# A conformer block on one core: another hand-fixed order for the first nine tenths of its instruction blocks, and the XN and AN clearings issued by VectorE

## The chip, the core and the metric

The kernel runs on one core of one Trainium2 chip. The time is that of one launch on the device, in microseconds (us). Before the change three runs gave 881.92, 882.08 and 883.56 us, median 882.08 us. The profile is that of one further execution of the same program.

In the text PE is TensorE (PEld its weight loads, which overlap its matmuls), ACT is ScalarE, DVE is VectorE, POOL is GpSimd and SP is SyncE, which here only issues DMAs.

## The reference, cut to what matters

Two sequences of 4000 tokens with 144 features go through one conformer block. All inputs are bf16.

```python
def reference(x, w_ff1a, w_ff1b, w_qkv, w_o, w_pw1, dw, w_pw2, w_ff2a, w_ff2b):
    B, T, D = x.shape                       # 2, 4000, 144; 4 heads of 36
    x = x + 0.5 * (_silu(_layernorm(x) @ w_ff1a) @ w_ff1b)
    qkv = _layernorm(x) @ w_qkv
    ...
    p = _softmax(jnp.einsum('bhqd,bhkd->bhqk', q, k) * scale, axis=-1)
    att = jnp.einsum('bhqk,bhkd->bhqd', p, v)
    ...
    x = x + att @ w_o
    h = _layernorm(x) @ w_pw1
    h = h[..., :D] * _sigmoid(h[..., D:])
    ...                                     # c: depthwise convolution over 5 tokens
    x = x + _silu(c) @ w_pw2
    x = x + 0.5 * (_silu(_layernorm(x) @ w_ff2a) @ w_ff2b)
    return _layernorm(x)
```

The softmax over 4000 keys for 4 heads and 8000 tokens is most of the work: 128 million exponentials.

## The kernel before

The 8000 tokens are cut into 16 chunks of 500, each of 4 blocks of 125 rows; 8 chunks make a sequence. Keys are cut into tiles of 64 rows, 62 full ones and one of 32 for a sequence. For a chunk of queries and a tile of keys, four matmuls on quarters of the PE array (64 rows by 64 columns; lines `PS<-QT,KT`) make scores for 4 heads in a pair of PSUM banks. ACT turns the pair into exponentials with one instruction (`PT<-PS 128x1000`). For every fifth tile or so DVE does it instead, with five instructions (two `PT<-PS 128x500`, two `PT<-PT` as integers, one product). Then four more quarter matmuls (`PS<-PT,VA`) multiply by the values and add up in two further banks. Six banks are left for scores and for all else.

Around this run, chunk by chunk: the first feed-forward layer, and the keys, values and queries, for the first sequence before and during its attention (the "front", the first 88 us or so); the rest for the second sequence beside the attention of the first; behind each chunk's attention the output projection, the gated convolution and the second feed-forward layer; at the end (the "tail", from some 836 us) what is left of the last chunks. A layer norm takes its statistics on DVE (`ST<-X`), the power -1/2 and, for most chunks, the normalisation itself on POOL (`RS`, `XN<-X,RS`). Its result XN is transposed on DVE in squares, written by SP's DMA queue to a scratch tensor `rows` and read back as XT or XTQ. XN and AN (the normalised and the attention rows, 5 and 4 buffers of 640 columns) have columns beyond the 576 that are ever written, and the transposes read them, so each buffer is cleared before its first use; so is the lower part of XT (5 buffers), 80 rows of which 16 come by DMA.

The order of all this is not left to a scheduler on the chip. The kernel's Python first emits operations greedily with a table of estimated costs; each decision of that loop is a step, and the operations of one engine in one step are a block. `Rec.reorder` (line 279) then moves the blocks of each engine: `ORDER` (line 38) is a string for each engine, in which a character says by how many places a block moves from its emitted place. `PLACES` (line 111) says, tile by tile, which of the six banks a PSUM tile takes; there are 1724 tiles. After that the semaphore waits are derived from the data dependencies in the final order (`Rec.finish`, line 344). So the four compute engines run four fixed lists, in order, that wait for each other by semaphores only: an instruction that waits holds up everything behind it on its engine.

The lines of the trace are nearly all those of `Rec.replay` (398), which issues every operation; groups are told apart by their tiles.

The clearings before: `ln` (line 1068) clears the 64 columns that matter on POOL at the first use of an XN buffer by halves of a chunk, and the whole buffer at its first use by a whole chunk; `setup_dw` (line 930) clears all AN at once on POOL when the front ends; `transp` (line 1038) clears XT's lower part on POOL at its first use by DMA. An emitted clearing also moves the greedy loop's clock on by its estimated cost, so that leaving it out would change what is emitted after it.

Of the kernel before, what the change touches and what calls it, by code (L numbers as in the profile page):

```python
# [39 lines left out]
        "PPPPPPQOQOPPPPPRPNPPQQQQLPPQORPNPRPTMORNNVO~OLNOMrMMNPMMNNNOMNNNOPLMQMMMNNPMMNSMNLMMOOPNSOMQMSPNOPU["  # L40
        "OMNRMOPPQIRMSNPNePNOOOcNNNNNNNNNOOLbNLOOQNSH]MMOLOMPMMOOOVPNOOOOPPPTOOOTPMUQMSLNNQQNQOQQNPPPPPTPPROK"
        "PPPPPPPPPPPP`PPPQKVPPKPPMPPRPUPPPROQQQRZOQQQRRKQRRSJPRRRRRRRWSZRNYUR~NHQ@R[KEGOOOPPPPKQOPPSPPSLPQMTP"
        "PPLQQQMPPPQVPPQOX_PTOPPCRTQQRGSQIQQSQRNV8OOQNNVSNOOLOPUUNN_MMWLNNRMMMMOOOPPPPPPQQNPPRSNRSSSORRVTR[OR"
        "AKQ@PPLOOQQNPPPPPUOOOOOPQOPPPPPUOOOOQRPLU`NNNXMMPNLQMNLZRNL`MN_YLLMK`KMNLILNQJMOOOPNYOPNOOOQNNZ^NNNN"
        "OOPNQNQOYP]CNNNNOMPMSO[NKOOQNVMPMMN`NbYMMMMNOMNIcLLNL[MMMNNQNRMJQLLROQSPLRNOQOPUQOMPQMPPRPVPLQOMQNPQ"
        "QQQSKPQSQKQQQQJPPPPPWQQSPKKQQUPPPSWPQRPQAVPPPQCVPQRPWHSYPHSOPQYPQEPQCPRZUPPSOOHDPR^OKOOOOPNOOOO^NOQN"
        "NOOOSNNNNS[NNNdRMNRKYNJWJNNNNNNGOOPP^YNNNNOMNNNNRNNPPPVROOLOOPPRZNNOOOOOPNOSOPNRPSMOOPQOQWNRPRLLNSZP"
        "NPQOIOQOTPPPRPQ]P^USPMMQIQKQQ8QTQQGMRRTQQKRRRRGLRSOMRPQQQJQQRPVP[OOOQEROO^IOQLNOOPPTTOMNQ[FOQNPPSPPM"
        "HPQOQQUPLOPNVPNOOSQNLUOOPNOXPPPLTQNLMPPPQOPPTOOPTPLOOQRNOPPPQOVPNOOOORZOP[PPMOOFRZOL[ROQKQTUBOKNFPPP"
        "_OOOOOOPNOOOOWNNVNNXMNTKMNOMZQOSLNOMSPSLLTPMOOUOPNOOTQOMOPPPQOPPPQOPPPTTQOSQSSSSNEEPQOPTPTMOMORSNNOP"  # L50
        "ROYPQOPQ^NPNPQOPAOOOOOSOOOPPPQQNPPPPPPXOOOOOOOaNPPPLOOOPUMOOOO[IOOPSOOQNPHPSWOOPPPPQGPPPPQQQMPPQQNPQ"
        "O_OOOPZOOOPI_NNNNZOPEOQWP^HKPHSJOLNOO`VPMRJOM^J`MPNKUNLUGNLJQNRIOPPRXOMOOOOPXMOPPMOOOPWOOPPPTKNOOPPP"
        "PPPPPPPQRPSYSQNQYZPRRRADIOXQGVOPJOORPIPPRRSSMR]MHOOQQQVRKNHPLPPPPPPPPPPRZQSQRRbHSGNQGPPQRRGLPQKQQQQJ"
        "QOQRPMQOPPQOSQNRMTROTNPXQQQEPJOQNPRPN_OPPPLRSOPLPPPGPPPSeOMPPQRJZPKLNNNN`NOKOVJNNNNcM`LMMMNNN]MNL]LL"
        "LLLLTWLXKMMVNQ_LMOPPQQ>MOOOTOMRbMMOOOOOTOOOQZIOPJMOOcOMPPT[PRORPEVHOPYCJQOQQGMOQQNQWNQNPPLSP_OaOOOPN"
        "PDPPPLOHPPQLPPPPQOTPNWNPPPWJNPPP`OIOPPPPPPPUQOELRP^TTQOZUPPCGOPQDJPPPPPPRPQWPRURPMFQQ_RPXDPQJLPNOJPN"
        "PPPPPSPPQ`PPTQQRERPQIQTNDPTPPJOPQQNPPUOPPSLPMPPRPQQRPJP[RNQQLaRJQSS[IQMGQQRPCZJPQOPQTPP@RPIPPPPQQQSS"
        "VXUQGNTQSSETDS`OQSCJQQdLOINQMRLLZMNSMMMMZLWPK]JMNLMTLNNNNVN`NNNNNROOPPJQOPLRPRMOQQRPLPXQQQRPTUQHFPQJ"
        "PPPPPPSPROUSPPTLPUOCOPNQOPROTWPRWRPVRZOY^YEOOPPMQ:;QDQQQQQQQQQEQQQMQOROVSMOTTQLVHROTRGNTVPHRPTRaJSQE"
        "QRSKNRNOQOPWQO=OOPNYOOOQNNOO]QOL_PNRO^NOUIPNK_MMW>MMMZMMMM]MMQLMMSNNOMOPPSOVNNPNXNPQOKQOQLQQQQUPPPHO"  # L60
        "QORPQMQOPQQSQOUVWNWMNOKOAOQOPPPPZWNNNOOLNNR^MNVNOMNNNNPSMN]NTNNNNNaNNNOQLN[RNOMRNHMSOSNPQGPQOPRXRPQW"
        "KOHOPPQYPPZPQRCO[I^NORFNNIZMMMNOWLNNNQMNRORRO_KPNOOOYNNNNNNOU^NSUHNKOJNOSOOQRJUPROTYMHNNURNNTMIPNQOU"
        "OOV[MNLNNNPYTNeJLNORNNGOO[]NNNNIQLMRLNRWOPUOO]OM`QO;LSOLO]JOJPRLLMRUNZMOVR[NPDOT^OOOFOSTOMNOSbPQLPRS"
        "_MORR_NPP^OHCNNNOZOWL~NHLMMNNNSOOXNOQQNSSOIVKPNPN]NOOOOOPPVOOOITNPPLPPQOWPPMRPNTKOOTNOPUMOOOQN`OOOPN"
        "OOPPPLOZOQQMPIQO^YROQQRLENO_PNPPPTQNNOROOSVO]QMNRNOPWTNOMNSOPQXbOOOQ[NO~NCdIMMMMMMMfbKMMMQMMJLMPLMUM"
        "MMNL^TR^JSLJQJUKPNLHQMPP`UNNNNOMOOOOPNOOPPPPQQNPQQQMUQQMSOPTQOPTPQUNQSPSQ<TRSSVEQQQHQQFPPPPPQSPMYTOL"
        "NNTMNNNP^[NOMNNQMMOLNN]PNOOR[OPKQN_ZLNESMOOKHOM[NPPLPNOOPPMQSTMNPQQQQRSQRRTCQVNGRNOMTTTMMNUPPQHNQSPM"
        "YVTQKLLSSOIJPSSPTMKORNOQOPPPPPPSORNSMRNRRRNQQRPFRPQQQQQQRPFQO"
    ),
    "act": (  # L70
        "PPPPPPPPPPPPPRSNNOSOOOPPPPPPPUPNOXNNOOOOOQNPPPPPPPPPROOPPQOPPPQOPPPPPPQQNPPPPPPPPPPPPPPPPPPPPPPPPPQO"
        "PPPPPPPPPPPPPPPPPPPPPPPPPPPPPPPPPPPPPPPPPPPPPPPPPPPPPPPPPPPPPPPPPPPPPPPPQOROSNOOPPPPPPPPPPPPPPPPPPPP"
        "PPPPPPPPPPPPPQOPPPPPPPPPPPPPPPPPPPPPPPPPQOPPQOPPPPPPPPPPPPPPPPPPPPPPPPPPPPPPPPPPPPPPPPPPPPPPPPPPPPPP"
        "PPPPPPPPPPPPPPPPPPPPPPPPPPPPPPPPPPPPPPPPPPPPPPPPPPPPPPPPPPPPPPPPPPPPPPPPPPPPPPPPPPPPPQOPPPPPPPPPPPPP"
        "PPPPPPPPPPPPPPPPPPPPPPPPPPPPPPQOPPQOPPPPPPPPPPPPPPPPPPPPPPPPPPPPPPPPPPPPPPPPPPPPROOPPQOPPPPPPPPPPPPP"
        "PPPPPPPPPPPPPPPPPPQOPPPPPPPPPPPPPPPPPPPPPPPPPQOQOPPPPPPPPPPPPPPPPPPPPPPPPPPPPPPPPPPPPPPPPPPPPPPPPPPP"
        "PPPPPPPPTOPNOPPPPPPPPPPPPPPPPPPPPPPPPPPPPPPPPPPPPPPPPPPPPPPPPPPPPPPPPPPQOPPPPQOPPPPPPPPPPPPPPPPPPPPP"
        "PPPPPPPPPPPPPPPPPPPPPPPPPPPPPPPPPPPPPPPROOPPQQNPPPPPPPPPPPPPPPPPPQOPPPPPPPQOPPPPPPPPPPPPPPPPPPPPPPPP"
        "PPPPPQOPPPPPPPPPPPPPPPPPROOPPPPPPPPPPPPPPPPPQOPPPPPPPPPPPPQOPPPPPPPPPPPPPPPPPPPPPPPPPPPPPPPPPPPPPPPP"
        "PQOPPPPPPPPPPPPQOPPPPPPPPPPPPPPPPPPPPPPPPPPPPPPPPPPPPPPPPPPPPPPPPPPPPPPPPPPQOPPPPPPPPPPPPPPPPPPPPPPP"  # L80
# [15 lines left out]
        "QOQOSPNOhQOPPPPPHOPNOPPQOROQNGOOPPPQOQOPQOPRPNPPPPQOPPPPPROTPPLQRULVOUOJPNJPPQOQOPRPQMPPPPPPPPQQQQQK"
        "QRNRNORPNUOUP[LNKPMRNRNLNQSSMRMRPKQOQQNQOWPPMQOXOPRPNSOWNCPNORNRTTPJSQMSPPQRZOROQQQQTPUHOPRO4PPPPPPQ"
        "QQRLRPQLPPPPPPPPPQOQQQMPPPPPQQQMPPPPPPPPPQQQSLTRPSQJQQQQQRTOPPRPRSQSQRRTQUPQTDO/OPS]NSMOLNQQNLOVQUPU"
        "OKHPLRRNNPPPQOPQRPQQQQVQOPQORSOP?PPPPPPPPPPPPRORPQQRPWQQNPTPUPUKOO<OPQOROQQMPQOPQQNPQQSPTQNPHPPROOQS"
        "NPQULPNOORROQRPJPPSOOORO]SOSNPRWQQXPTRERGRRTTUXRTRSBSSSSSSSSAT@S&NNPPPPPPPPPPQO"  # L100
    ),
    "pool": (
        "PPPPPPRPNPPPROOPPPSOOOPPPPPQQNPQOPPPYOOOOO[NNNR`NNJOMSMMOMOXOOLNOOUORLOMROQQQRPSIOOPPSOOOPQRNOPPPTOO"
        "PNPPPPVOOPNOQNPPPRPQM"
    ),
    "sp": (
        "PPPPPPPPQOPPPPPPPPPPPPPPSOTNNOOPPPQOPPPROQNPPPPPPPPPPPPPQOPPQOQOPPPPPPPPPPPPPPQOPPPPPVOPNSNNQMPPPQOP"
        "ROYNOOOPNOOUNTNOMNPPPSOOOPPPPPPPPPPPPPQOQOPPPPQQN"
    ),
}  # L110
PLACES = (
    "4540352315301235404310523035204320244354321123203214052534114030254011540241204124012410314032034023"
    "4203423041304302402430243203420342040324304023420342034203420342034203420342034203420342034040254012"
# [26 lines left out]

def c_act(n):
    return n / 1200 + 0.053


class Op:
    __slots__ = ("eng", "name", "a", "k", "idx", "deps", "clock", "inc", "waits", "cnt", "q", "done", "t0", "t1", "kind", "step", "tile", "shared", "own", "acc", "base")


class Place(int):
    pass  # L150


# [1953 lines left out]
```

## Time and profile before

| | |
|---|---|
| median of three runs | 882.08 us |
| the profiled execution, first to last instruction (its span) | 880.5 us |
| instructions in the trace | 27000 |
| HBM traffic | 13.44 MB read, 13.61 MB written |
| DMA engines, mean rate | 33 GB/s |

The trace gives a start and a duration for each instruction. [...] A row that ends in a bracket such as `[2.21 <-PE PS L398]` says how long the engine was idle before it and whose semaphore ended that.

The chain of waits starts at the last instruction and goes back, at each step, to what released it or, if it waited for nothing, to the one before it on its engine. Its shares by engine say where a shorter instruction would have brought the end forward.

### The profile page before, as it was taken

What the parts mean: (1) busy time and instruction counts of PE and PEld (TensorE: products, weight loads), DVE (VectorE), ACT (ScalarE), POOL (GpSimd) and SP (SyncE); (2) the same over time, 40 slices, a digit from 0 to 9 for tenths busy, and PEclk for the clock granted to TensorE, in tenths of its full rate; (3) what the DMA queues carried; (4) which work ended last, traced back from release to release, by engine and by line L of the source; (5) the groups of instructions that cost most, each with busy time, mean ns of one, the idle gap of its engine ahead of it and who ended that gap; (6) DMA issues with size and microseconds to landing.
All of it is one profiled execution on the core that took longest, in us unless ns stands there. A gap on an engine that the chain in (4) does not pass through costs nothing.

```text
span 880.5 us, 27000 instructions
## 1 busy us (share of the span) xinstructions
PE 851.5 (97%) x11419; PEld 380.2 (43%) x11419; DVE 822.7 (93%) x1812; ACT 849.6 (96%) x1098; POOL 300.4 (34%) x584
## 2 busy tenths in 40 slices
PE   8998999999999999999999999999999999999996
PEld 6543433344444443443444444344443433444366
DVE  7977999999999999999989999899999999999987
ACT  6799999999999999999999999999999999999986
POOL 7770331431336130252111813522513404032434
PEclk9999999999999999999999999999999999999999
DMA  3221001220221110212001120110110011001111
GB/s 100 44 55 38 16 18 36 62 51 16 40 49 38 23 38 22 45 24 45 16 9 30 36 44 23 23 26 20 43 31 18 21 37 20 17 12 36 27 27 33
DMA packets 114351, 28.80 MB, mean 33 GB/s; under 512 B 101090, under 2 KB 114230, under 8 KB 114230
## 3 DMA queue, kind: packets, MB, share of 16 engines
q1 hardware_dynamic: 112646, 26.39, 13.8%
q8 instruction: 89, 1.46, 0.7%
q10 hardware_dynamic: 1584, 0.69, 0.3%
q14 instruction: 32, 0.26, 0.1%
HBM read 13.44 MB, written 13.61 MB: 31 GB/s over the span
## 4 chain that ended last, share of the span: by engine, by line
ACT 46%; PE 33%; DVE 17%; POOL 2%; DMA 1%; issue 1%; SPq 1%; POOLq 0%; DVEq 0%
ACT PT L398 42%; PE PS L398 33%; DVE PT L398 7%; ACT TH L398 4%; DVE HT L398 2%; DVE ST L398 2%; DVE X L398 2%; DVE XN L398 2%; POOL RS L398 1%; POOL XN L398 1%; DVE KT L398 1%; DVE QT L398 1%; DVE AN L398 1%; SPq L398 1%; DMA rows<-XN 0%
## 5 line engine op out<-in xcount | busy, mean ns | idle before, releaser
L398 ACT ACTIVATE PT<-PS 128x1000 bf16<-128x1000 f32 (+1 forms) x818 | 757.2, 1074 | 4.1 <-PE PS L398 2.4
L398 PE MATMUL PS<-QT,KT 64*64 64x500 bf16 x3968 | 425.7, 385 | 13.0 <-ACT PT L398 5.2
L398 PE MATMUL PS<-PT,VA 64*37 64x500 bf16 x4728 | 411.5, 372 | 1.8 <-DVE QT L398 0.7
L398 DVE TENSOR_SCALAR PT<-PS 128x500 int16<-128x500 f32 x380 | 250.1, 668 | 5.8 <-PE PS L398 3.9
L398 PEld LDWEIGHTS PS<-QT,KT 64*64 64x64 bf16 x3968 | 123.4, 104 | 236.8 <-ACT PT L398 137.1
L398 POOL TENSOR_SCALAR RS<-ST 125x4 f32<-125x4 f32 x130 | 37.0, 284 | 482.2 <-DVE ST L398 475.6
L398 PEld LDWEIGHTS PS<-PT,VA 64*37 64x37 bf16 x4728 | 141.4, 96 | 96.2 <-DVE PT L398 18.7
L398 DVE TENSOR_SCALAR PT<-PT 128x1000 uint16<-128x1000 uint16 x380 | 154.5, 418 | 2.1 <-PE PS L398 0.8
L398 POOL TENSOR_SCALAR XN<-X,RS 125x144 bf16<-125x144 bf16 x260 | 150.4, 610 | 13.1 <-DMA out_dram<-XN 6.4
L398 DVE TENSOR_TENSOR PT<-PT 128x1000 bf16<-128x1000 bf16 x190 | 128.8, 679 | 1.3
L398 ACT ACTIVATE TH<-PS 128x500 bf16<-128x500 f32 (+3 forms) x194 | 107.3, 575 | 7.4 <-PE PS L398 6.5
L398 POOL TENSOR_TENSOR RS<-RS,NHALF 125x4 f32<-125x4 f32 (+1 forms) x93 | 91.7, 989 | 33.1 <-DVE RS L398 27.3
L398 DVE SCALAR_TENSOR_TENSOR HT<-TH,PS 128x500 bf16<-128x500 bf16 (+1 forms) x135 | 81.2, 615 | 12.8 <-ACT TH L398 12.0
L398 PE MATMUL PS<-XT,WA 80*128 80x500 bf16 (+5 forms) x288 | 74.5, 365 | 2.2 <-DMA XT<-rows 0.9
L398 DVE BATCH_NORM_STATS2 ST<-X 125x6 f32<-125x288 bf16 x160 | 65.7, 447 | 2.8 <-DMA X<-in_x_dram 2.7
L398 DVE SCALAR_TENSOR_TENSOR X<-PS,X 125x288 bf16<-125x288 f32 (+1 forms) x128 | 56.6, 449 | 6.5 <-PE PS L398 5.2
L398 PE MATMUL PS<-WB,HT 128*125 128x144 bf16 (+1 forms) x640 | 52.4, 230 | 0.7 <-ACT HT L398 0.5
L398 PEld LDWEIGHTS PS<-WB,HT 128*125 128x125 bf16 (+1 forms) x640 | 44.3, 136 | 14.5 <-issue 3.8
L398 PEld LDWEIGHTS PS<-XT,WA 128*128 128x128 bf16 (+1 forms) x288 | 21.2, 97 | 38.8 <-issue 10.6
L398 PE MATMUL PS<-U,DG 128*128 128x250 bf16 (+6 forms) x204 | 29.6, 264 | 0.0
L398 DVE STREAM_TRANSPOSE XN<-XN 128x320 f32<-128x320 f32 x54 | 27.0, 500 | 1.0 <-POOL XN L398 1.0
L398 POOL COPY U<-U 128x2 bf16<-128x2 bf16 (+1 forms) x54 | 9.2, 209 | 46.3 <-DVE U L398 46.3
(95 smaller groups left out, 522.6 us busy)
## 6 DMA issues: line engine op xcount, KB each, us to landing
rows<-XN SPq DMA_DIRECT2D x216, 40.0 KB, 2.0
XT<-rows SPq DMA_DIRECT2D x56, 128.0 KB, 2.0
rows<-AN SPq DMA_DIRECT2D x60, 40.0 KB, 2.0
X<-in_x_dram SPq DMA_DIRECT2D x15, 140.6 KB
XTQ<-rows SPq DMA_DIRECT2D x26, 70.3 KB
out_dram<-XN SPq DMA_DIRECT2D x13, 140.6 KB
XT<-rows SPq DMA_DIRECT2D x56, 16.0 KB, 1.9
out_dram<-XN SPq DMA_DIRECT2D x3, 70.3 KB
```

Of the source, the lines that this page charges most:

```text
L398: ins = getattr(eng, o.name)(*o.a, **o.k)
```

## The change

Three things change; the emitted operations and the machinery are otherwise the same.

1. New strings in `ORDER` for all five engines, and new banks in `PLACES`. The emitted blocks are the same as before, with the same steps, and only the places they move to differ. In the last part of each list the places are those of before: the last 652 matmuls, 107 ACT, 152 DVE and 51 POOL instructions stand in the same order in both programs. Ahead of that 2284 of PE's 2855 blocks stand elsewhere, by 3.4 places on average and 31 at most, 170 of ACT's 1093 blocks by at most 10 places, 1035 of DVE's 1680 by at most 24, 62 of POOL's and 64 of SP's. Of the 1724 PSUM tiles 278 have another bank.

2. XN and AN are cleared by VectorE, a buffer at a time, in nine blocks that are emitted ahead of everything and are then moved by `ORDER`. Where POOL cleared them, a "ghost" is emitted: it costs the greedy loop what the clearing did, and `reorder` takes it out and hands its dependencies on.

3. XT is cleared in three columns of 128 (`TB:128`) for those buffers that a transpose on PE has filled before; the two others are cleared as before.

```diff
@@ ORDER, PLACES: new strings @@
     def reorder(self, table):
+        real = {}
+
+        def through(o):
+            if id(o) not in real:
+                ds = {}
+                for d, raw in o.deps:
+                    for x, how in through(d) if d.ghost else [(d, raw)]:
+                        if x is not o:
+                            ds[id(x)] = (x, how or ds.get(id(x), (x, None))[1])
+                real[id(o)] = list(ds.values())
+            return real[id(o)]
+
+        for o in self.ops:
+            drop = o.shared - o.own
+            o.deps = [(d, raw) for d, raw in o.deps if id(d) not in drop]
+        for o in self.ops:
+            if any(d.ghost for d, raw in o.deps):
+                o.deps = through(o)
+        self.ops = [o for o in self.ops if not o.ghost]
...
+    def side(like, *a, **k):
+        kept = dict(R.free), R.kind, R.last, R.filling
+        R.filling = True
+        o = op(*a, cost=0.0, **k)
+        R.free, R.kind, R.last, R.filling = kept
...
+    def early(j, what, w):
+        side(None, "dve", "memset", what, 0.0, w=w).step = j / 64
+
+    for u in range(NXN):
+        early(1 + u, XNS[:, u, :], [("XN", u)])
+    for a in range(NAN):
+        early(21 + a, ANS[:, a, :], [("AN", a)])
...
     def setup_dw():
-        op("pool", "memset", ANS[:, :, :], 0.0, w=[("AN", a) for a in range(NAN)], cost=2.2)
+        op("pool", "ghost", w=[("AN", a) for a in range(NAN)], cost=2.2)
...
         if dma and s not in xt_set:
             xt_set.add(s)
-            op("pool", "memset", XT[0:LP, s, 1, :, :], 0.0, w=wk, cost=0.5)
+            whole = all((s, i) in xt_whole for i in range(NB))
+            op("pool", "memset", XT[0:LP, s, 1, :, TB:128] if whole else XT[0:LP, s, 1, :, :], 0.0, w=wk, cost=0.5)
...
-            op("pool", "memset", XNS[:, u, :] if inter else XNS[:, u, n * D:n * D + 64], 0.0, w=[("XN", u)], cost=0.56)
+            op("pool", "ghost", w=[("XN", u)], cost=0.56)
...
-            op("pool", "memset", XNS[:, u, :], 0.0, w=[("XN", u)], cost=0.0)
+            op("pool", "ghost", w=[("XN", u)], cost=0.0)
```

In instructions: POOL loses five clearings of XN in part, five of XN whole and the one of AN, and three of its five XT clearings shrink from 512 columns to 12. DVE gains nine clearings of 128 x 640 bf16, issued as 128 x 320 words. Nothing else is added or removed.

More of the change, by code (lines that the diff above doesn't have):

```diff
@@ L45 @@
[L45 to L59, printed above, removed]
@@ new lines @@
+    "2405420524052450240524052504250425042505250424052405320552504202503103215541240124210412041204131043"
+    "1034015320330515301035153010351304024302430243014320431043024301340342034203421034301540132034021402"
+    "1402140214021402140214143134021402140214021402140204112042104310431043104012430154301240124240214214"
+    "0134021402140210421041204120412041302423003424302431043024302420342503034020412142104214124021402140"
+    "2140214021401340214020412040214031041204120412140134013402140204120402141124021402015240240524052052"
@@ L145 @@
 class Op:
-    __slots__ = ("eng", "name", "a", "k", "idx", "deps", "clock", "inc", "waits", "cnt", "q", "done", "t0", "t1", "kind", "step", "tile", "shared", "own", "acc", "base")
+    __slots__ = ("eng", "name", "a", "k", "idx", "deps", "clock", "inc", "waits", "cnt", "q", "done", "t0", "t1", "kind", "step", "tile", "shared", "own", "acc", "base", "ghost")
 class Place(int):
@@ L868, in bass_standalone__conformer_family_zipformer__speech_kernel @@
     op("pool", "memset", WK[:, :, :, :], 0.0, w=["WK0"], cost=0.3)
+    def side(like, *a, **k):
[3 more added lines that the diff above has]
+        R.free, R.kind, R.last, R.filling = kept
+        if like is not None:
+            o.done = like.done
+        return o
+    def early(j, what, w):
[4 more added lines that the diff above has]
+        early(21 + a, ANS[:, a, :], [("AN", a)])
     def setup_v():
@@ L1048, in transp @@
             return
+        if not inter:
+            xt_whole.update((s, i) for i in bs)
         bk = yield need("pe", banks, dur=0.11 * n)
```

137 lines of the change are left out of this document (74 added, 63 removed).

## The prediction

> **What bounds the kernel now.** I read the page's busy shares and chain first, then the busy time of each engine by stage, then ACT's groups by shape in the stage that is longest.
>
> ```profile
> PE 851.5 (97%) x11419; PEld 380.2 (43%) x11419; DVE 822.7 (93%) x1812; ACT 849.6 (96%) x1098; POOL 300.4 (34%) x584
> ACT 46%; PE 33%; DVE 17%; POOL 2%; DMA 1%; issue 1%; SPq 1%; POOLq 0%; DVEq 0%
> 0.00:22.00 22.00, 18.47 (x221) 15.09 (x225) 15.90 (x63) 13.93 (x30) 15.66 (x43) 1.00 0.40 100
> 22.00:44.00 22.00, 20.03 (x207) 11.67 (x207) 21.02 (x55) 16.15 (x30) 16.89 (x34) 1.00 0.21 44
> 44.00:88.00 44.00, 41.28 (x534) 16.40 (x532) 32.37 (x65) 42.25 (x56) 15.57 (x30) 1.00 0.21 47
> 88.00:616.00 528.00, 519.97 (x7067) 219.85 (x7069) 503.01 (x1066) 524.19 (x645) 170.31 (x325) 1.00 0.15 31
> 616.00:792.00 176.00, 170.94 (x2353) 71.78 (x2349) 170.91 (x359) 175.85 (x216) 50.32 (x95) 1.00 0.11 25
> 836.00:881.00 45.00, 37.85 (x452) 28.07 (x448) 37.05 (x121) 33.31 (x73) 16.35 (x31) 0.96 0.12 31
> ```
>
> The window rows give, after the stretch and its length, busy time and count of PE, PEld, DVE, ACT and POOL, then the granted clock. Three engines are nearly full at once, and the chain passes between them: 46% ACT, 33% PE, 17% DVE. POOL is on it for 2%. The clock is 1.00 except in the tail, so no time is lost there.
>
> Busy time overstates ACT, so I work out its load from spacings: 30 exponentials in one piece of the chain take 26.51 us, 0.884 each, though the groups below give one a mean of 1070 ns.
>
> ```profile
> 781.83 26.51 ACT PT L398 x30
> 79.35 0.48 ACT TH L398
> 85.69 0.27 ACT TH L398
> L398 ACT ACTIVATE PT<-PS 128x1000 bf16<-128x1000 f32 x523 | 490.3, 1070 | 3.0 <-PE PS L398 1.5
> L398 ACT ACTIVATE TH<-PS 128x500 bf16<-128x500 f32 x78 | 51.1, 669 | 0.0
> L398 ACT ACTIVATE TH<-PS 128x250 bf16<-128x250 f32 x15 | 7.4, 492 | 0.1
> L398 ACT ACTIVATE PT<-PS 128x500 bf16<-128x500 f32 x11 | 7.1, 649 | 0.0
> L398 ACT ACTIVATE TH<-PS 64x125 bf16<-64x125 f32 x10 | 2.7, 274 | 0.6 <-PE PS L398 0.4
> L398 ACT ACTIVATE TH<-PS 80x125 bf16<-80x125 f32 x8 | 2.4, 294 | 0.0
> by line: ACT PT L398 93.2%; ACT TH L398 7.2%; issue 0.1%
> ```
>
> The groups are those of 88 to 616 us; the last row is the chain's shares from 616 to 792 us. In 88 to 616 us: 523 x 0.884 + (78 + 11) x 0.48 + 15 x 0.27 + 2.7 + 2.4 = 462.3 + 42.7 + 4.1 + 5.1 = 514.2 us of 528. **ACT loses 13.8 us there**, in gaps that its busy row hides (524.19). From 616 us to the end of the main run the chain is ACT alone; a better order finds nothing there. In the front ACT is idle 8.07, 5.85 and 1.75 us in the first three rows; in 22 to 44 us DVE is the full one (21.02 of 22).
>
> So the bound is ACT's list, about 2.6% away from full in the long stage, with PE close behind; what an order can win is a part of 13.8 us and a part of the front.
>
> **The change part by part.** *The clearings.* POOL loses five whole XN buffers, five parts, AN, and most of three XT clearings.
>
> ```profile
> L398 POOL MEMSET XN<- 128x640 bf16 x5 | 3.2, 630 | 0.0
> L398 POOL MEMSET XN<- 128x64 bf16 x5 | 0.5, 145 | 0.0
> L398 POOL MEMSET AN<- 128x2560 bf16 x1 | 2.2, 2227 | 0.0
> L398 POOL MEMSET XT<- 80x512 bf16 x5 | 2.6, 519 | 0.0
> L398 POOL TENSOR_SCALAR RS<-ST 125x4 f32<-125x4 f32 x130 | 37.0, 284 | 482.2 <-DVE ST L398 475.6
> L398 DVE MEMSET KL<- 128x128 uint32 x1 | 0.2, 165 | 0.0
> L398 DVE MEMSET WA<- 80x256 uint32 x1 | 0.3, 272 | 0.8 <-PEq L2091 0.8
> L398 DVE MEMSET WPZ<- 128x176 uint32 x1 | 0.2, 205 | 0.0
> L398 DVE MEMSET DG<- 128x120 uint32 x1 | 0.2, 158 | 0.0
> 3.91 0.46 DVE L398 BATCH_NORM_STATS2 ST<-X 125x6 f32<-125x288 bf16 x1 [2.09 <-DMA X<-in_x_dram]
> 67.77 0.68 DVE L398 TENSOR_SCALAR QT<-PS 128x500 bf16<-128x500 f32 x1 [2.21 <-PE PS L398]
> 71.01 1.26 DVE L398 SCALAR_TENSOR_TENSOR HT<-TH,PS 128x500 bf16<-128x500 bf16 x2 [1.98 <-ACT TH L398]
> 32.85 1.39 POOL L398 TENSOR_TENSOR RS<-RS,NHALF 125x2 f32<-125x2 f32 x2 [2.06 <-DVE RS L398]
> ```
>
> POOL is relieved of 3.2 + 0.5 + 2.2 us and, with 12 columns priced between nothing and the 145 ns of the 64-column row, of 3 x 0.4 = 1.2: 7.1 us. It waits 475.6 us for DVE's statistics anyway. Only three XN clearings, ahead of the first whole chunks, lie in a stretch without waits, which ends in the idle 2.06 us at 32.85; they are worth 0 to 3 x 0.63 = 1.9 us.
>
> On DVE no clearing of 320 words is shown. From 128 words (165 ns) and 256 (272) it is 0.84 ns a word, so 0.33 us, nine of them 3.0 us. In DVE's new list three XN clearings stand, with those of WPZ and DG, ahead of the first statistics, where DVE now idles 2.09 us for X: 3 x 0.33 + 0.21 + 0.16 = 1.36, covered. The fourth and fifth follow the second statistics and the first normalised rows, in place of the WPZ and DG clearings that stood between the first statistics: even. The four AN clearings stand among the copies of KT and VA before DVE's first exponential, in the stretch with idle 2.21 and 1.98. I take 0; with all cover gone 3.0.
>
> *The order.* ACT's and DVE's work is the same instructions. On PE I counted the changes between quarter-array matmuls and the others in both lists: 797 before, 793 after. A change has this price:
>
> ```profile
> 299.25 0.59 PE L398 MATMUL PS<-XTQ,WQ 72*128 72x500 bf16 x2
> 299.78 0.41 PE L398 MATMUL PS<-QT,KT 64*64 64x500 bf16 x4
> L398 PE MATMUL PS<-XTQ,WQ 72*128 72x500 bf16 x60 | 17.9, 379 | 0.1
> 401.18 0.38 PE L398 MATMUL PS<-PT,VA 64*37 64x500 bf16 x4
> 405.26 0.60 PE L398 MATMUL PS<-PT,VA 64*37 64x500 bf16 x8
> PEld PS L398 <- ACT PT L398: 87.1, 243, 0.8
> ```
>
> Two of 379 ns in 0.59 start 0.21 apart, a third would start at 299.67, the scores start at 299.78: 0.11 us. Four fewer are -0.4 us. The Trainium skill (TensorEngine Tiling, Key Properties) says that a change of tiling mode drains TensorE; read as the whole of a matmul's 0.38 us it would make the term -1.5 us. The trace shows the smaller price.
>
> What the new order does to the waits I read from the lists: for each ACT instruction, how many matmuls must be done, through all dependencies, before it can start. Among the 645 ACT instructions of 88 to 616 us, 471 need fewer than before, 62 more, on average 5.4 fewer. Four quarter matmuls add 0.60 - 0.38 = 0.22 us, so what ACT waits for is ready 5.4/4 x 0.22 = 0.30 us sooner in PE's list. The price is on the other side: PE's instructions in this stage need on average 0.49 more ACT results, so 0.49 x 0.884 = 0.43 us less slack on the banks and exponentials they wait for. And the loop has not grown: an ACT instruction and the latest one that its matmuls had to wait for stand 2.68 ACT instructions apart before, 2.64 after. The order spends slack of PE's line, which has some where ACT is the chain and none where PE is, to feed ACT sooner.
>
> How much of the 13.8 us this closes the trace can't show. The bounds are all of it, and a loss of 0.43 us at a part of the 243 waits of the last row. I take a quarter, 3.5 us: nearer to nothing, since PE is on the chain for much of this stage.
>
> For the front, between a loss of 3.0 (the clearings uncovered) and a gain of 5.85 (ACT's idle time of 22 to 44 us), I take 1.0: DVE holds that stretch and its work there is the same.
>
> **Sum** against the profiled span: 880.5 - 3.5 - 1.0 - 0.4 = 875.6 us. The median of the runs is 1.6 above the span (882.08 - 880.5): **877.2 us**.
>
> **The rivals.** *A larger gain.* Half of the 13.8 and 3 us of the front: 882.1 - 6.9 - 3.0 - 0.4 = 871.8. For it speaks how one-sided the 471 to 62 is; against it that DVE, too, is 503 of 528.
>
> *Nothing.* The loop's length decides (2.68 and 2.64), ACT's gaps only change places: 882.1 - 0.4 = 881.7.
>
> *Slower: PE's line pays.* At each of the 243 waits of PE for an ACT exponential in 88 to 616 us, a tenth of the 0.43 us comes onto the path, since PE, behind the wait, has the value products and the layers' matmuls queued that DVE and the next chunks wait for: 243 x 0.043 = 10.4 us, against the gains of 4.9: 882.1 + 10.4 - 4.9 = 887.6. It decides from 0.02 us a wait on. For it speaks PE's 519.97 of 528; against it that these waits, 0.36 us on average (87.1/243), are there now and the chain passes most of them by.
>
> *Slower: the clearings are not covered* because X lands before DVE is through, or PE's matmuls come sooner in the stretch of the AN clearings, and the order brings nothing: 882.1 + 3.0 = 885.1.
>
> *The change doesn't do what it says* I take as excluded for the last part: the ends of the lists are the same, 652 matmuls and 107 ACT instructions, of which the last window row shows 452 and 73 behind 836 us. Where they begin, just ahead of that, another order has gone before; I put the joint at nothing, with no row to price it.
>
> **How the numbers follow.** My forecast 0.42, the larger gain 0.17, nothing 0.12, PE's line pays 0.21, clearings uncovered 0.08. About 0.2%, 1.8 us, is what a measurement of this kernel can tell from no change. So faster 0.59, same 0.12, slower 0.29. The range is 870 to 889: it takes in the larger gain and both slower cases and leaves out a gain of over two thirds of what can be gained and a PE line that pays more than worked out; the forecast's own range is 873 to 880.
>
> **What would show it.** Right: ACT's spacing sum of the long stage (514 us of work) now fits in some 524; the first-sequence stretch up to ACT's 616 us mark ends 4 to 5 us sooner; the wait of PEld for ACT's exponentials grows from 87.1 us without the chain's PE share growing; DVE's wait of 2.09 us for X shrinks to under 1. Wrong: PE's share of the chain grows past 33%, or ACT's gaps stay at 13.8 us; a DVE clearing of much over 0.33 us or one in the chain of the front; time lost behind 836 us.

## The result, and the profile after

The changed kernel took **880.07 us** (median of 16 runs, 879.16 to 881.69), the kernel before 882.12 us on the same chip (16 runs, 881.06 to 883.56). The ratio is 0.9979, 95% interval 0.9972 to 0.9986: 2.05 us faster, by the interval 1.2 to 2.5 us. The forecast was 4.9 us faster. The direction held, and the time lies inside the range, but the gain is less than half of what was forecast.

The page of the changed kernel gives the busy shares and the shares of the chain of waits; the windows are those of before, with the same columns.

```profile
PE 846.0 (96%) x11419; PEld 385.3 (44%) x11419; DVE 824.1 (94%) x1821; ACT 849.8 (97%) x1098; POOL 293.9 (33%) x573
ACT 49%; PE 29%; DVE 16%; POOL 3%; DMA 1%; issue 1%; SPq 0%; ACTq 0%; POOLq 0%; DVEq 0%
0.00:22.00 22.00, 17.70 (x215) 14.26 (x215) 17.98 (x70) 13.95 (x30) 14.58 (x38) 1.00 0.39 99
22.00:44.00 22.00, 20.76 (x196) 11.00 (x194) 20.40 (x50) 17.43 (x32) 15.36 (x32) 1.00 0.26 52
44.00:88.00 44.00, 43.10 (x591) 19.47 (x590) 36.35 (x77) 43.77 (x57) 11.93 (x26) 1.00 0.19 44
88.00:616.00 528.00, 518.07 (x7086) 224.48 (x7083) 503.18 (x1067) 525.01 (x647) 177.19 (x333) 1.00 0.15 31
616.00:792.00 176.00, 168.75 (x2343) 71.34 (x2343) 169.69 (x356) 175.76 (x215) 42.40 (x82) 1.00 0.12 25
836.00:881.00 45.00, 34.67 (x405) 26.63 (x403) 33.72 (x115) 29.93 (x69) 16.35 (x31) 0.95 0.10 26
```

The reader is to see how little has moved. Between 88 and 616 us ACT starts 647 instructions instead of 645. In 22 to 44 us ACT's busy time rises from 16.15 to 17.43 and DVE's falls from 21.02 to 20.40. From 616 to 792 us, where ACT alone was the chain, ACT starts one instruction fewer (215, was 216), PE does 10 matmuls fewer and DVE three instructions fewer.

ACT's groups of 88 to 616 us, by shape, give the same sum as in the prediction.

```profile
L419 ACT ACTIVATE PT<-PS 128x1000 bf16<-128x1000 f32 x524 | 485.6, 1052 | 2.0 <-PE PS L419 1.1
L419 ACT ACTIVATE TH<-PS 128x500 bf16<-128x500 f32 x79 | 48.0, 624 | 0.8 <-PE PS L419 0.6
L419 ACT ACTIVATE PT<-PS 128x500 bf16<-128x500 f32 x11 | 7.0, 634 | 0.0
L419 ACT ACTIVATE TH<-PS 128x250 bf16<-128x250 f32 x15 | 6.8, 455 | 0.0
L419 ACT ACTIVATE TH<-PS 64x125 bf16<-64x125 f32 x10 | 2.7, 274 | 0.2
L419 ACT ACTIVATE TH<-PS 80x125 bf16<-80x125 f32 x8 | 2.3, 283 | 0.0
PEld PS L419 <- ACT PT L419: 90.0, 259, 0.9
```

524 x 0.884 + (79 + 11) x 0.48 + 15 x 0.27 + 2.7 + 2.3 = 515.5 us of work stand in the same 528 us. ACT loses 12.5 us there, and lost 13.8: the long stage has given **1.3 us**, not 3.5. The last row is from the waits of that stage: PE's wait for ACT's exponentials went from 87.1 us in 243 waits to 90.0 in 259.

Behind it, in the chain's shares from 616 to 792 us, something is new. Before, this row had ACT at 93.2 and 7.2% and nothing else.

```profile
by line: ACT PT L419 74.5%; PE PS L419 9.4%; DVE PT L419 7.9%; ACT TH L419 6.7%; DVE AN L419 0.5%; DVE X L419 0.4%; DVE XN L419 0.4%; issue 0.3%; DVE SW L419 0.1%; DVE RD L419 0.1%
```

So the new order has let PE and DVE onto a path that ACT had held alone as far as 792 us. (Over 616 to 836 us the chain of before has PE at 6.3%.)

Last the clearings: the groups of DVE's two new ones, and DVE's timeline around the first statistics.

```profile
L419 DVE MEMSET XN<- 128x320 uint32 x5 | 1.6, 325 | 0.2
L419 DVE MEMSET AN<- 128x320 uint32 x4 | 1.3, 325 | 0.1
1.93 1.01 DVE L419 MEMSET XN<- 128x320 uint32 x3
2.92 0.20 DVE L419 MEMSET WPZ<- 128x176 uint32 x1
3.10 0.16 DVE L419 MEMSET DG<- 128x120 uint32 x1
3.82 0.46 DVE L419 BATCH_NORM_STATS2 ST<-X 125x6 f32<-125x288 bf16 x1 [0.56 <-DMA X<-in_x_dram]
```

325 ns each, as estimated (0.33), and DVE still waits 0.56 us for X behind three of them: they are covered.

### The profile page after: what moved, and what is told of

It reads as the page before. It is cut to its first block, busy times and chain, and to the rows that moved or that the text cites. A ratio compares the mean times of both kernels' runs of the same rounds, so it can differ in the third digit from the quotient of the medians.

```text
span 878.1 us, 27043 instructions
## 1 busy us (share of the span) xinstructions
PE 846.0 (96%) x11419; PEld 385.3 (44%) x11419; DVE 824.1 (94%) x1821; ACT 849.8 (97%) x1098; POOL 293.9 (33%) x573
## 3 DMA queue, kind: packets, MB, share of 16 engines
q1 hardware_dynamic: 112646, 26.39, 13.8%
## 4 chain that ended last, share of the span: by engine, by line
ACT 49%; PE 29%; DVE 16%; POOL 3%; DMA 1%; issue 1%; SPq 0%; ACTq 0%; POOLq 0%; DVEq 0%
ACT PT L419 45%; PE PS L419 29%; DVE PT L419 7%; ACT TH L419 4%; DVE ST L419 2%; POOL XN L419 2%; DVE HT L419 2%; POOL RS L419 2%; DVE XN L419 1%; DVE X L419 1%; DVE QT L419 1%; DMA X<-in_x_dram 0%; DMA XT<-rows 0%; DMA WE<-in_w_ff1a_dram 0%; DVE KT L419 0%
## 5 line engine op out<-in xcount | busy, mean ns | idle before, releaser
L419 PE MATMUL PS<-QT,KT 64*64 64x500 bf16 x3968 | 420.0, 384 | 15.4 <-ACT PT L419 8.7
L419 PE MATMUL PS<-PT,VA 64*37 64x500 bf16 x4728 | 403.1, 372 | 0.7 <-DVE QT L419 0.4
L419 POOL TENSOR_SCALAR RS<-ST 125x4 f32<-125x4 f32 x130 | 39.8, 306 | 484.3 <-DVE ST L419 478.0
L419 DVE TENSOR_SCALAR PT<-PT 128x1000 uint16<-128x1000 uint16 x380 | 152.7, 417 | 2.2 <-PE PS L419 1.0
L419 POOL TENSOR_SCALAR XN<-X,RS 125x144 bf16<-125x144 bf16 x260 | 146.8, 594 | 8.3
L419 ACT ACTIVATE TH<-PS 128x500 bf16<-128x500 f32 (+3 forms) x194 | 101.7, 543 | 5.2 <-PE PS L419 4.3
```

Source lines behind the costliest of these rows:

```text
L419: ins = getattr(eng, o.name)(*o.a, **o.k)
```

## The experiments

Fifteen experiments were run beside the kernel before on the same chip: five runs each of e11_less_act, e15, e16 and e17, four of e9_lead, eleven of each of the others. The table has them in the order of the text; e13 and e14 repeat the changed kernel and e4_to616.

| kernel | us | before, same chip | ratio, 95% interval |
|---|---|---|---|
| e1_clears | 881.76 | 881.66 | 1.0002 (0.9993 to 1.0011) |
| e2_order | 881.45 | 881.66 | 1.0002 (0.9994 to 1.0011) |
| e3_front | 881.17 | 881.66 | 0.9996 (0.9987 to 1.0004) |
| e4_to616 | 879.67 | 881.66 | 0.9982 (0.9973 to 0.9990) |
| e7_mid | 880.81 | 881.16 | 0.9995 (0.9986 to 1.0004) |
| e8_late | 882.74 | 881.16 | 1.0018 (1.0008 to 1.0027) |
| e13_changed_again | 879.63 | 881.42 | 0.9986 (0.9977 to 0.9995) |
| e14_to616_again | 880.09 | 881.42 | 0.9987 (0.9978 to 0.9996) |
| e9_lead | 929.36 | 881.16 | 1.0546 (1.0532 to 1.0561) |
| e10_less_pe | 880.58 | 881.16 | 0.9992 (0.9983 to 1.0001) |
| e11_less_act | 877.88 | 881.42 | 0.9964 (0.9951 to 0.9978) |
| e12_less_dve | 880.25 | 881.42 | 0.9990 (0.9981 to 0.9999) |
| e15_less_all | 875.27 | 881.41 | 0.9932 (0.9919 to 0.9944) |
| e16_less_act_dve | 875.59 | 881.41 | 0.9932 (0.9920 to 0.9945) |
| e17_less_act_pe | 876.62 | 881.41 | 0.9946 (0.9932 to 0.9960) |

Since the four lists are fixed, the n-th instruction of ACT can be compared between traces. The second table is worked out from the traces: the start of ACT's n-th instruction less that start in the profiled execution of before, in us. Differences between two columns say what a stretch gave or cost.

| ACT's instruction (before, us) | 110 (85.4) | 740 (602.8) | 758 (616.4) | 1025 (835.1) |
|---|---|---|---|---|
| changed kernel | -3.04 | -4.32 | -4.65 | -3.37 |
| e13_changed_again | -1.78 | -2.94 | -3.25 | -1.87 |
| e1_clears | -1.08 | -0.54 | -0.49 | -0.35 |
| e2_order | -1.24 | -2.52 | -2.84 | -1.59 |
| e3_front | -2.31 | -2.05 | -2.04 | -2.03 |
| e4_to616 | -3.33 | -4.60 | -4.13 | -3.97 |
| e14_to616_again | -2.84 | -3.98 | -3.52 | -3.36 |
| e7_mid | -0.52 | -2.26 | -1.81 | -1.66 |
| e8_late | -1.07 | -0.85 | -1.17 | +0.22 |
| e10_less_pe | -1.11 | -1.79 | -1.78 | -1.76 |
| e11_less_act | +0.76 | -1.40 | -1.15 | -2.62 |
| e12_less_dve | -0.80 | -2.11 | -2.10 | -2.09 |
| e15_less_all | -0.28 | -4.20 | -3.96 | -6.32 |

The first column says least. The changed kernel itself has -3.04 in one execution and -1.78 in another, and three traces with the old front and whole work (e1_clears, e7_mid, e8_late) have -0.52 to -1.08, where the profiled execution of before has 0. In the traces of e13_changed_again, e2_order and e11_less_act the granted clock is at half for 3.41 us of the front (shown in the last section), so their first numbers are to be set beside each other, not beside the rest.

**The clearings and the order apart.** e1_clears has the old strings and banks with the clearings on DVE, each in DVE's list beside the instructions that it stands beside in the changed kernel. e2_order has the new strings and banks with the clearings on POOL.

```diff
@@ e1_clears: before, and of the change only @@
+        early(1 + u, XNS[:, u, :], [("XN", u)])
+        early(21 + a, ANS[:, a, :], [("AN", a)])
@@ e2_order: before, and of the change only @@
 ORDER = { new strings }
 PLACES = ( new banks )
```

> The clearings alone: XN and AN cleared by VectorE at the places that they have in the changed kernel, XT's narrower clearing, every other block in the order and banks of before. Theory (the clearings are covered and POOL's relief is worth little): within 0.5 us of before, with DVE's idle time for X shorter by the three XN clearings. Rival (the 2.5 us that the front of the changed kernel gains come from POOL's relief): 2 to 2.5 us faster than before. Second rival (the clearings are not covered): up to 3.0 us slower.

> The order and banks alone: POOL clears XN, AN and XT as before, all other blocks stand as in the changed kernel. Theory (the order brings the gain): 1.5 to 2.5 us faster than before, as the changed kernel. Rival (the new order of the front needs POOL's relief): no faster than before, and the time is lost in the first 88 us.

In the launch's time neither does anything alone: both intervals lie around 1 (1.0002 each; one run of e2_order at 884.80 us pulls its ratio up), while the changed kernel's ends at 0.9986. So by the runs most of the gain needs both. Two things narrow this. By the median span e2_order is 0.6 us shorter than the kernel before (879.3 and 879.9 us), but its launches take 2.22 us over the span, those of the kernel before 1.80. And from ACT's instruction 110 to 740 its trace gains 1.28 us, as the changed kernel's does. So the long stage's gain needs the order alone, and what the clearings add lies in the front (-1.24 and -1.78 us at instruction 110, both with the clock at half) or outside the span. What they do in the front, POOL's timeline shows, first of the changed kernel, then of e2_order, then of the kernel before. Rows between these are left out, and the views end at 34 us, so the last group of e2_order shows three of its four rows.

```profile
21.64 1.04 POOL L419 TENSOR_TENSOR RS<-RS,NHALF 125x4 f32<-125x4 f32 x1
27.64 2.31 POOL L419 TENSOR_SCALAR XN<-X,RS 125x144 bf16<-125x144 bf16 x4
29.86 0.12 POOL L419 MEMSET XT<- 80x12 bf16 x1
30.34 1.04 POOL L419 TENSOR_TENSOR RS<-RS,NHALF 125x4 f32<-125x4 f32 x1
31.78 2.34 POOL L419 TENSOR_SCALAR XN<-X,RS 125x144 bf16<-125x144 bf16 x4
```

```profile
22.27 1.04 POOL L398 TENSOR_TENSOR RS<-RS,NHALF 125x4 f32<-125x4 f32 x1
28.37 1.87 POOL L398 TENSOR_SCALAR XN<-X,RS 125x144 bf16<-125x144 bf16 x4
30.14 0.52 POOL L398 MEMSET XT<- 80x512 bf16 x1
30.60 0.63 POOL L398 MEMSET XN<- 128x640 bf16 x1
31.58 1.04 POOL L398 TENSOR_TENSOR RS<-RS,NHALF 125x4 f32<-125x4 f32 x1
33.05 1.42 POOL L398 TENSOR_SCALAR XN<-X,RS 125x144 bf16<-125x144 bf16 x3
```

```profile
26.08 0.63 POOL L398 MEMSET XN<- 128x640 bf16 x1
28.50 1.86 POOL L398 TENSOR_SCALAR XN<-X,RS 125x144 bf16<-125x144 bf16 x4
30.27 0.52 POOL L398 MEMSET XT<- 80x512 bf16 x1
32.85 1.39 POOL L398 TENSOR_TENSOR RS<-RS,NHALF 125x2 f32<-125x2 f32 x2 [2.06 <-DVE RS L398]
```

In the old order POOL has whole chunks to normalise, then stands idle for 2.06 us; a clearing less only makes it idle longer. In the new order another whole chunk follows at once, without a wait, so each clearing lies on POOL's own line: from the first power to the third it takes 30.34 - 21.64 = 8.70 us without and 31.58 - 22.27 = 9.31 us with them. This shows 0.6 us of the difference between e2_order and the changed kernel, which is 1.8 us by the medians (0.21 and 2.05 us under the kernel before beside them). Another 0.4 us is e2_order's longer time outside the span, with a cause that its trace doesn't show. Where the rest comes from is open.

**Where along the run.** e3_front and e4_to616 have the changed kernel up to a block of PE's list (at about 88 and 614 us) and the old order and banks behind it. e7_mid has the new order only between these two blocks, e8_late only behind the second. All have DVE's clearings.

```diff
 ORDER = { "pe", "act", "dve", "pool", "sp": each
-  new order throughout
+  e3_front:  new | old | old       (cut at about 88 and 614 us)
+  e4_to616:  new | new | old
+  e7_mid:    old | new | old
+  e8_late:   old | old | new
 }
```

> The changed kernel's order, banks and clearings up to some 88 us of the trace, the order and banks of before behind that. Theory (the front's gain is real and lasts, since ACT is the chain later): 2 to 2.5 us faster than before, ACT's instructions behind 88 us all earlier by that much. Rival (what the front gains is waited away before 616 us, where PE and DVE hold the chain for half of the time): within 0.5 us of before.

> The changed kernel's order, banks and clearings up to some 614 us, the order and banks of before behind that, so that the stretch in which ACT alone was the chain has its old order. Theory (the changed kernel gains 4.6 us up to here, and its new order gives 1.3 us back between 616 and 836 us): 3.5 to 4.5 us faster than before, 1 to 2 faster than the changed kernel. Rival (the 1.3 us are given back in any order, since the queries and layers of the last chunks come late): as the changed kernel, 2 us faster than before.

> The changed kernel's order and banks from 88 to 614 us alone; the order and banks of before ahead of that and behind it, the clearings on VectorE. Theory (the order's gain comes from the long stage, some 1.5 us of it, and the front brings 0.4 as in the run with the new front alone): 1.2 to 2 us faster than before. Rival (the new middle needs the state that the new front leaves): within 0.5 us of before.

> The order and banks of before up to 614 us, those of the changed kernel behind that; the clearings on VectorE. Theory (ACT alone is the chain behind 614 us and the new order opens gaps there): 0.5 to 1.3 us slower than before. Rival (the late part is even, and what the trace of the changed kernel lost there is the spread of one execution): within 0.4 us of before.

The front alone gives 0.5 us (from 1.1 faster to 0.4 slower), the middle alone 0.35 us (1.2 faster to 0.4 slower), front and middle together 2.0 (0.9 to 2.4), and the late part alone *costs* 1.6 us (0.7 to 2.4), 0.25 of it outside the span. So e3_front and e7_mid came out as their rivals had it, and e4_to616 missed the 3.5 to 4.5 us of its theory. The parts alone make 0.85 us and together 2.0; the intervals are too wide to say that they don't add up. The second table agrees on the signs. From instruction 110 to 740 all six traces with the new middle gain: 1.28 (the changed kernel), 1.16, 1.28, 1.27, 1.14, and 1.74 in e7_mid. Three with the old middle and whole work (e1_clears, e3_front, e8_late) lose 0.54, 0.26 and 0.22 against the profiled execution of before. From 740 to 1025 the new late order loses 0.95, 1.07, 0.93 and 1.07 us in four traces. The old late order loses 0.19 and 0.02 in e1_clears and e3_front; where it follows the new middle it loses 0.60 to 0.63, most of it at the joint, instruction 758. The chain's shares from 616 to 792 us show what differs, first of e8_late, then of e4_to616.

```profile
by line: ACT PT L419 74.5%; PE PS L419 9.4%; ACT TH L419 6.7%; DVE PT L419 6.3%; POOL XN L419 1.3%; POOL RS L419 0.7%; DVE AN L419 0.5%; DVE X L419 0.4%; DVE XN L419 0.3%; issue 0.3%; DVE SW L419 0.1%; DVE RD L419 0.1%
by line: ACT PT L419 93.2%; ACT TH L419 7.0%; issue 0.1%
```

With the new late order PE and DVE are on the chain behind the old front and middle too; with the old one they are not, behind the new front and middle either (most in e1_clears: PE 2.1%).

That made e4_to616 the candidate to beat both kernels. It was run again beside the changed kernel.

> The changed kernel as it is, on the same chip and beside the same runs as the next kernel. As measured: 1.7 to 2.5 us faster than before, span 878.1 to 878.4.

> The changed order up to 614 us and the old order and banks behind it, once more. If the new order loses 0.95 us between 616 and 835 us, as the starts of ACT's instructions in the traces say, and the old one does not, this is 2.5 to 3.2 us faster than before and about 0.9 us faster than the changed kernel. If the joint eats that up, the two are the same within 0.3 us.

It doesn't beat it: 880.09 and 879.63 us. Its median span, 877.5 us, is the shorter (877.7 for the changed kernel), but the launch's time is 2.37 us above the span in the median, 1.84 for the changed kernel, and 1.80 for the kernel before. The traces' DMA packets show what stands in that time. In the trace of e14_to616_again a packet of 16384 bytes of an instruction queue (q8, kind "instruction" in the page's list of DMA queues) begins 2.26 us after the last instruction of the program and ends 3.15 us after it; that launch took 2.91 us over its span. In e4_to616's trace such a packet ends at 2.70 us, with 2.46 over the span, and in e8_late's one of 8192 bytes (q14) at 2.25, with 2.02. In all three the packet's end is 0.23 or 0.24 us more than the time over the span. In the changed kernel's two traces no packet ends later than the last instruction, and the time over the span is 1.87 and 1.81. So the launch seems to wait there for instructions to be fetched; no run varied that. e2_order's trace, with 2.25 over the span, has no such packet. So the loss of the late part is shown by e8_late's runs and by four traces; putting the old order back shortens the median span by only 0.2 us, and the launch loses more than that behind it.

**Does sooner help?** The forecast's long-stage term rested on a count: 471 ACT instructions need fewer matmuls. e9_lead makes that count better by force for the score exponentials, at the price of the instructions whose matmuls the scores pass. In the old order, 513 of the 536 groups of score matmuls between 88 and 614 us go one block earlier in PE's list, past 4.4 matmuls each on average, with nothing else moved.

```diff
 ORDER = { "pe":
-  ..., other block, score block, ...
+  ..., score block, other block, ...     (513 times)
 }
```

> The order and banks of before with the clearings on VectorE; between 88 and 614 us 513 of the 536 groups of score matmuls stand one block earlier in PE's list than before, passing 2239 matmuls, 4.4 each; ACT's, DVE's, POOL's and SP's lists as before. Theory by which the prediction costed the order (scores that come sooner in PE's list close ACT's gaps): 1.5 to 3.5 us faster than before. Rival (the gaps are not a matter of this lead: PE stalls sooner on the banks, and what it put off comes late for DVE and ACT): no faster, 0 to 6 us slower.

It is 48.2 us slower. The rows are of e9_lead, its window of the long stage and three of its waits there.

```profile
88.00:616.00 528.00, 496.56 (x6472) 200.68 (x6468) 466.18 (x974) 490.59 (x589) 158.07 (x307) 1.00 0.14 29
PEld PS L419 <- ACT PT L419: 105.9, 223, 1.5
ACT TH L419 <- PE PS L419: 21.4, 58, 0.9
ACT PT L419 <- PE PS L419: 12.9, 32, 1.0
```

PE's wait for exponentials takes 105.9 us in 223 waits, up to 1.5 us each (0.9 in the changed kernel). Behind that wait PE holds what the layers' ACT instructions (TH) and other exponentials need, and ACT now waits 21.4 + 12.9 us for PE. The same view of the kernel before has 1.9 us:

```profile
ACT PT L398 <- PE PS L398: 1.5, 4, 0.6
ACT TH L398 <- PE PS L398: 0.4, 1, 0.4
```

ACT starts 589 instead of 645 instructions. The bank or the exponential that a score needs isn't there sooner because the score stands sooner: 48.2/513 = 0.09 us lost a group. So here a count of matmuls ahead of an ACT instruction is no measure of time.

**What does hold the long stage?** Three kernels take work off one engine each, in the old order. e10_less_pe multiplies 20 of 500 columns by the values for every twelfth key tile (the sums lack those terms); e11_less_act works out 250 of 500 columns a bank for every twentieth key tile, where ACT has it; e12_less_dve does three operations on half the columns for every sixth exponential of DVE.

```diff
@@ e10_less_pe @@
+        w = 20 if n % 12 == 5 and n > 60 else CH
-               lhsT=..., rhs=PT[64 * p:64 * p + 64, pt, hh, :],
+               lhsT=..., rhs=PT[64 * p:64 * p + 64, pt, hh, 0:w],
@@ e11_less_act @@
+        w = CH // 2 if n % 20 == 7 and n > 60 else CH
-        exps.append(op("act", "activation", PT[:, pt, :, :], PSV[:, lo:hi + 1, 0:CH], ACT.Exp, bias=0.0,
+        exps.append(op("act", "activation", PT[:, pt, :, 0:w], PSV[:, lo:hi + 1, 0:w], ACT.Exp, bias=0.0,
@@ e12_less_dve @@
+        w = CH if stats["dve"] % 6 == 1 else 2 * CH
-        zu, yu = (PTU[:, q, :, :].rearrange("p b n -> p (b n)") for q in (z, y))
+        zu, yu = (PTU[:, q, :, :].rearrange("p b n -> p (b n)")[:, 0:w] for q in (z, y))
```

> The kernel of before with less work on PE: the value products of every twelfth key tile take 20 columns instead of 500 (their sums are left out), some 95 groups of four, near 0.15 to 0.2 us each, 9 to 13 us of PE's work between 88 and 616 us and 14 to 19 us in all. Theory (PE's amount of work is a bound of the long stage beside ACT's, so no order could have closed all of ACT's 13.8 us): a third or more of what is taken from PE in that stage, 3 to 5 us, comes off the time there. Rival (the stage is bound by waits and ACT alone): under 1 us comes off.

> The kernel before, but every twentieth ACT exponential tile behind the front is worked out on 250 of the 500 columns of each bank, about 0.42 us less each by the 0.884 us spacing of the whole ones, some 11 us less ACT work in 88 to 616 us; the other columns keep what their buffer held. Theory A (ACT's amount of work sets the pace of the long stage, the gaps stay): 9 to 11 us faster. Theory B (the pace is set by the hand-overs between the three engines, none of the three alone): 2 to 6 us faster, and ACT's gaps grow by the rest. Theory C (PE or DVE sets the pace): under 2 us faster, as with the value products made short.

> The kernel before, but every sixth exponential tile that DVE works out does its two bit operations and its product on 500 of 1000 columns, about 0.5 us less each, some 10 us less DVE work in 88 to 616 us; the other columns keep what their buffer held. Theory A (ACT's work sets the pace): within 1 us of the kernel before. Theory B (hand-overs): 1 to 4 us faster, since DVE's part of the chain in this stage gets shorter. Theory C with DVE as the pace: 7 to 10 us faster.

The next rows are the sums of busy time over the windows of the whole run, first of the kernel before, then of e10_less_pe, then of e11_less_act with two of its ACT groups of 88 to 616 us and the chain of its page, then the sum of e12_less_dve.

```profile
sum 881.00, PE 851.46 PEld 380.17 DVE 822.75 ACT 849.62 POOL 300.44; mean PE 121.64 PEld 54.31 DVE 117.54 ACT 121.37 POOL 42.92
```

```profile
sum 881.00, PE 845.37 PEld 375.33 DVE 822.48 ACT 848.92 POOL 301.80; mean PE 120.77 PEld 53.62 DVE 117.50 ACT 121.27 POOL 43.11
```

```profile
sum 881.00, PE 850.41 PEld 381.62 DVE 821.51 ACT 840.90 POOL 301.73; mean PE 121.49 PEld 54.52 DVE 117.36 ACT 120.13 POOL 43.10
L398 ACT ACTIVATE PT<-PS 128x1000 bf16<-128x1000 f32 x501 | 471.0, 1045 | 6.1 <-PE PS L398 4.4
L398 ACT ACTIVATE PT<-PS 128x500 bf16<-128x500 f32 x35 | 22.4, 641 | 0.5 <-PE PS L398 0.4
PE 41%; DVE 31%; ACT 23%; DMA 2%; POOL 1%; issue 1%; SPq 1%; ACTq 0%; POOLq 0%; DVEq 0%
```

```profile
sum 881.00, PE 850.38 PEld 380.56 DVE 810.75 ACT 848.75 POOL 298.17; mean PE 121.48 PEld 54.37 DVE 115.82 ACT 121.25 POOL 42.60
```

Against the first row PE is busy 6.1 us less in e10_less_pe, ACT 8.7 in e11_less_act, DVE 12.0 in e12_less_dve. The time fell by 0.6, 3.5 and 1.2 us. So a microsecond of busy time taken off PE is worth about 0.1, off DVE 0.1, off ACT 0.4. On PE and ACT, whose instructions overlap, busy time understates what was taken off. By spacings ACT has 35 short exponentials more in the whole run, 35 x (0.884 - 0.48) = 14.1 us less to do, and a microsecond is worth 0.25. On PE four short products take 0.03 us to the next matmul's start and four whole ones 0.21 (medians), so the 85 short groups save some 15 us by this estimate, worth 0.04 each. By either measure none of the three is the bound alone, and the shares of the chain (46, 33 and 17%) promised more than came. In the long stage ACT has 35 - 11 = 24 short exponentials more, 24 x (0.884 - 0.48) = 9.7 us less to do; its instructions 110 to 740 come closer together by 0.76 + 1.40 = 2.2 us only, and some of that may be time made up from its late front. ACT's idle time before whole exponentials grew from 3.0 to 6.1 us, and its share of the chain fell from 46 to 23% while PE's and DVE's rose. Theory B, the hand-overs, fits this run; theory A would have been 9 to 11 us.

That left two ways: the next engine takes up what one gives (then all three shortened together give more than their sum), or the hand-overs themselves hold the stage (then the sum, or less). The last three kernels combine the edits.

> The kernel before with all three shortenings of the earlier runs at once: every twelfth key tile's value products on 20 of 500 columns, every twentieth ACT exponential on 250 of 500 columns a bank, every sixth DVE exponential's three operations in SBUF on 500 of 1000 columns. Alone they were 0.6, 3.5 and 1.2 us faster, 5.3 together. Theory S (the pace is shared: when one engine is relieved, the next one holds): clearly more than the sum, 8 to 12 us faster. Theory L (each hand-over costs what it costs, whatever the engines have to do): the sum or less, 4 to 6 us.

> The kernel before with the short ACT exponentials and the short DVE operations, PE's work whole. Alone 3.5 and 1.2 us faster, 4.7 together. Theory S with PE as the next to hold: under 4.7, since PE keeps its whole work. Theory S with DVE as the next to hold: 6 to 8 us. Theory L: about 4.7.

> The kernel before with the short ACT exponentials and the short value products, DVE's work whole. Alone 3.5 and 0.6 us faster, 4.1 together. Theory S with PE as the next to hold: 6 to 8 us. Theory S with DVE as the next to hold: under 4.5. Theory L: about 4.1.

They gave 6.1, 5.8 and 4.8 us against sums of 5.3, 4.7 and 4.1. The three excesses of 0.7 to 1.1 us lie inside the intervals, each of which is about 1.2 us wide to either side, and are far from the 8 to 12 us that theory S expected of the first. In the long stage e15_less_all gives -0.28 + 4.20 = 3.9 us, against 0.7, 2.2 and 1.3, 4.2 together, for its parts. So the gains add up, as if each shortened tile helped where the path passes through it and nowhere else. Theory L stands, with two reserves: e16_less_act_dve's interval (4.9 to 7.1 us) reaches into what theory S expected with DVE as the next to hold, so that e15_less_all alone speaks clearly against S; and a shortened tile in twelve, twenty or six is a sparse test, and a kernel with every tile shortened was not run.

## Why the prediction had the direction right and the size wrong

*The clearings, taken as 0.* Right as to their price: 325 ns, covered by DVE's wait for X (0.56 us left of 2.09), and e1_clears moves nothing. The forecast missed that POOL's relief, worth nothing in the old order, is worth something in the new front: 0.6 us by POOL's rows, up to 1.3 by the median spans (0.6 us under the kernel before in e2_order, 1.9 in e13_changed_again).

*The front, -1.0 us.* Not settled: e3_front has -0.5 with an interval that holds both 0 and -1.0, and the traces of the new front vary by 1.3 us between executions of one kernel. The 1.0 was a choice between two wide bounds, so that a hit would have been luck.

*The long stage, a quarter of ACT's 13.8 us, -3.5 us.* **This is the step that failed**, and it is a size: the gaps are now 12.5 us, and the starts of ACT's instructions say 1.28 and 1.16 us in the changed kernel's two traces, a tenth instead of a quarter; against the three other traces of the old middle it is 1.4 to 1.8, about half of 3.5 at most. Two things were wrong behind the fraction. First, the gaps were read as room for an order, since ACT was read as the bound with PE close behind. e11_less_act shows that even 9.7 us taken off ACT shorten the stage by 2.2: read with e15_less_all, the gaps are hand-overs among three lists, and come back elsewhere. Second, the argument for a quarter was the count of matmuls ahead of ACT's instructions; e9_lead puts the scores still further ahead and loses 48 us. The rival that PE's line pays named the mechanism that e9_lead shows, at 0.09 us a group moved (the rival took 0.043 a wait); the new order mostly avoids it (90.0 us of waits for 87.1), so it did not decide.

*The late part, taken as 0* because ACT alone was the chain and a better order finds nothing there. The new order is worse there: ACT's 100% of the chain fell to 81%, and ACT's instructions 740 to 1025 lose about 1 us in four traces; e8_late has it alone at +1.6 us. A stretch in which one engine had no gaps had nothing to gain here and something to lose, and it should have been priced as a loss.

*The changes between array modes, -0.4 us,* were not measured apart. The 797 and 793 count every change between matmuls of up to and over 64 rows or columns. Those between quarter matmuls and all others, which the 0.11 us is a price of, fall from 776 to 762 in the traces' order, which would make -1.5 us.

Put together from the second table, long stage and late part make 1.28 - 0.95 = 0.33 us against the profiled execution of before, which leaves most of the 2.05 to the front, where e3_front's runs alone show 0.5. That split stays open; that the long stage, forecast to bring seven tenths, brought less does not. Of what was to show it right, the mark at 616 us did come 4.65 us sooner in the profiled execution, but 3.04 of that was there at 85 us, and part of that is the difference between executions; PE's share of the chain did not grow (33 to 29%). ACT's gaps, named as the sign of a failure, stayed at nine tenths of what they were.

## What to carry to other kernels

Where three in-order engines are all busy for 93% and more, as here, don't take idle time on one of them for room: first take a per cent or two of work off each engine in turn and see what the time does. Here a microsecond off PE or DVE gave 0.1 us or less and off ACT 0.25 to 0.4, so there was little room. Judge a new order by where its waits fall, not by how many instructions stand ahead of a consumer, and price the stretches that have no slack as losses. Two edits that each show nothing in the launch's time can show a gain together; one reason seen here is that the first moves a line of work onto an engine's path and the second shortens it there. Read the span beside the launch's time: they moved by up to 0.6 us against each other here.

## What was not expected of the hardware

The start of the run differs between executions of one kernel, and the granted clock goes with it. The first window of the changed kernel's second trace has a granted clock of 0.92 where the first trace has 1.00: for 3.41 us of it the clock is at half.

```profile
0.00:22.00 22.00, 18.26 (x205) 15.17 (x205) 15.78 (x63) 11.85 (x27) 13.95 (x36) 0.92 0.37 99
16.41:19.82 3.41, 3.41 (x21) 2.40 (x19) 2.55 (x8) 2.08 (x6) 2.94 (x6) 0.50 0.43 98
```

ACT starts 27 instructions there, and 30 in the first trace, and from its instruction 110 on it stays 1.3 to 1.5 us later up to 835 us (-1.78 and -3.04, -1.87 and -3.37). The traces of e2_order (15.43 to 18.84 us) and e11_less_act (15.66 to 19.07) have the clock at half in the front too, the other fourteen don't. ACT's instruction 30 starts at 24.00 to 24.96 us in these three and at 21.53 to 23.22 in the fourteen. What lowered the clock the traces don't say. Behind the front the traces repeat to some tenths of a microsecond, so a change of 1 us can be read between two instructions of one trace when it can't be read from the start.

The first normalised rows on POOL stand further apart where DVE has cleared their buffers: four take 2.31 us in the changed kernel, 1.86 in the kernel before and 1.87 in e2_order (rows above), though each instruction lasts about 0.50 us in all of them. That gives back some 0.45 of the 0.63 us that a clearing took. The cause was not tried.
